# Float32 weights made from float64 by their bits: work moved from VectorE to ScalarE, in blocks of 1024 columns

## Chip, cores and metric

One core of one Trainium2 chip. The metric is device time in microseconds (us) of one execution, median of several; lower is better. All runs quoted here were in the fast state. Engine names as in the profile: PE is TensorE's matmuls, PEld its weight loads, DVE is VectorE, ACT is ScalarE, POOL is GpSimd, SP is SyncE, which issues most transfers here.

## The reference, cut to what matters

Two attention reads (tokens from state, state from tokens) feed a feed-forward block with ELU. The weights arrive as 8-byte words, float64.

```python
def _attn_ref(x, state):            # x 8 x 8 x 512 x 64, state 8 x 8 x 32 x 64
    scores = scale * x @ state^T;   a  = softmax(scores);   xread = a  @ state
    scores2 = scale * state @ x^T;  a2 = softmax(scores2);  sread = a2 @ x
    return concat([xread, sread], axis=2)

def _moe_ref(x, w_in, w_out):       # x 4352 x 512, w_in 512 x 2048, w_out 2048 x 512
    h = x @ w_in
    g = np.where(h > 0.0, h, np.exp(np.minimum(h, 0.0)) - 1.0)
    return g @ w_out
```

## The kernel before

A float64 word is loaded as two 32-bit words, `lo` and `hi`. DVE rebuilds the float32 value with seven instructions per block of 512 columns; there are 16 blocks of w_in and 16 of w_out.

```python
    rawpool = ctx.enter_context(tc.tile_pool(name="raw", bufs=3))
    ...
    w_in = cpool.tile([P, NP, DF], FP32, name="w_in")
    w_out = cpool.tile([P, FO, DM], FP32, name="w_out")
    v_bd = cpool.tile([P, B * G, P], FP32, name="v_bd")
    k_bd = cpool.tile([P, B * G, P], FP32, name="k_bd")
    ...

    def setup():
        nc.vector.memset(v_bd, 0.0)
        make_identity(nc, ident)
        s_v = state.rearrange("b (g h) n d -> h n (b g) d", h=4)
        for h in range(4):
            c = h % 2
            nc.gpsimd.dma_start(
                out=v_bd[h * NS : (h + 1) * NS, :, c * D : (c + 1) * D], in_=s_v[h]
            )
        for b in range(2):
            load_x(b)
        for k in range(0, B * G, 4):
            ps = bank([P, 4, P], "k_ps")
            for i in range(4):
                nc.tensor.transpose(ps[:, i], v_bd[:, k + i], ident)
            nc.vector.tensor_copy(out=k_bd[:, k : k + 4], in_=ps)
    ...
    def load_weights(dst, src):


        raw = rawpool.tile([P, 512], moe_w_in.dtype, name="raw")
        k = src.shape[-1]
        nc.sync.dma_start(out=raw.rearrange("p (j k) -> p j k", k=k), in_=src)
        words = raw.bitcast(U32).rearrange("p (j k w) -> p j k w", k=k, w=2)
        lo, hi = words[:, :, :, 0], words[:, :, :, 1]
        power = wpool.tile([P, 512], U32, name="power").rearrange("p (j k) -> p j k", k=k)

        nc.vector.tensor_scalar(
            out=power, in0=hi, scalar1=20, scalar2=0x7FF,
            op0=ALU.logical_shift_right, op1=ALU.bitwise_and,
        )
        low = 1023 - 127
        nc.vector.tensor_scalar(
            out=power, in0=power, scalar1=float(low), scalar2=float(low + 255),
            op0=ALU.max, op1=ALU.min,
        )
        nc.vector.tensor_scalar(
            out=power, in0=power, scalar1=float(-low), scalar2=float(1 << 23),
            op0=ALU.add, op1=ALU.mult,
        )
        nc.vector.scalar_tensor_tensor(
            out=power, in0=hi, scalar=0x80000000, in1=power,
            op0=ALU.bitwise_and, op1=ALU.bitwise_or,
        )

        nc.vector.tensor_scalar(
            out=hi, in0=hi, scalar1=0xFFFFF, scalar2=0x100000,
            op0=ALU.bitwise_and, op1=ALU.bitwise_or,
        )
        nc.vector.scalar_tensor_tensor(
            out=dst, in0=lo, scalar=2.0**-32, in1=hi, op0=ALU.mult, op1=ALU.add
        )
        nc.vector.scalar_tensor_tensor(
            out=dst, in0=dst, scalar=2.0**-20, in1=power.bitcast(FP32),
            op0=ALU.mult, op1=ALU.mult,
        )
```

Its users: `make_m` multiplies k_bd with one chunk (512 columns) of w_in, two rows of the tile per m_ps bank, and `ffn1` of a batch needs m for its chunk; `ffn2` needs w_out.

```python
        for g in range(G):
            ps = bank([P, 512], "m_ps")
            for i in range(2):
                nc.tensor.matmul(
                    ps[i * D : (i + 1) * D],
                    k_bd[:, b * G + g, i * D : (i + 1) * D],
                    w_in[:, 2 * g + i, c * 512 : (c + 1) * 512],
                    start=True, stop=True,
                )
    ...
    setup()
    todo = [lambda c=c, n=n: load_w_in(c, n) for c in range(FC) for n in range(NP)]
    for f in attention(0):
        f()
        if todo:
            todo.pop(0)()
    ...
    make_m(0, 0)
```

The order of instructions in each engine's queue is not the order of this text: it is fixed at compile time, so an edit in one place can also move instructions elsewhere (w_out_cheap below shows a case). Names that end in `_ps` are tiles in PSUM; every matmul of this kernel writes one, `h_ps` in `ffn1` and `o_ps` in `ffn2`.

Of the kernel before, what the change touches and what calls it, by code (L numbers as in the profile page):

```python
# [2 lines left out]

# [6 lines left out]
FP32 = mybir.dt.float32  # L10
I32 = mybir.dt.int32
U32 = mybir.dt.uint32
AX_X = mybir.AxisListType.X
AF = mybir.ActivationFunctionType
ALU = mybir.AluOpType
PSUM = bass.MemoryType.PSUM


@with_exitstack
def kernel(  # L20
# [11 lines left out]
    nc = tc.nc  # L32

    B, H, S, D = x.shape
    NS = state.shape[2]
    DM, DF = moe_w_in.shape
    P = 128
    R = S // P
    NP = H // 2
    G = H // 4  # L40
    FO = DF // P
    FC = DF // 512
    SB = S + NS
    NB = S // 32
    scale = 1.0 / math.sqrt(D)
# [7 lines left out]
    w_in_v = moe_w_in.rearrange("(co ci) f -> ci co f", ci=P)  # L53
    w_out_v = moe_w_out.rearrange("(fo fi) c -> fi fo c", fi=P)

    cpool = ctx.enter_context(tc.tile_pool(name="const", bufs=1))
# [2 lines left out]
    xtpool = ctx.enter_context(tc.tile_pool(name="xT", bufs=4))  # L59
    atpool = ctx.enter_context(tc.tile_pool(name="aT", bufs=4))  # L60
    mpool = ctx.enter_context(tc.tile_pool(name="m", bufs=2))
    rawpool = ctx.enter_context(tc.tile_pool(name="raw", bufs=3))
    wpool = ctx.enter_context(tc.tile_pool(name="pow", bufs=2))
    small = ctx.enter_context(tc.tile_pool(name="small", bufs=4))
    gpool = ctx.enter_context(tc.tile_pool(name="g", bufs=FO + 1))
# [1 line left out]
    opool = ctx.enter_context(tc.tile_pool(name="o", bufs=2))  # L67
    ps_a = ctx.enter_context(tc.tile_pool(name="ps_a", bufs=3, space=PSUM))
    ps_h = ctx.enter_context(tc.tile_pool(name="ps_h", bufs=3, space=PSUM))
    ps_o = ctx.enter_context(tc.tile_pool(name="ps_o", bufs=2, space=PSUM))  # L70

# [7 lines left out]
    w_in = cpool.tile([P, NP, DF], FP32, name="w_in")  # L79
    w_out = cpool.tile([P, FO, DM], FP32, name="w_out")  # L80


    v_bd = cpool.tile([P, B * G, P], FP32, name="v_bd")

    k_bd = cpool.tile([P, B * G, P], FP32, name="k_bd")

# [12 lines left out]
# [17 lines that stand above are left out]
    def load_weights(dst, src):  # L116


        raw = rawpool.tile([P, 512], moe_w_in.dtype, name="raw")
        k = src.shape[-1]  # L120
        nc.sync.dma_start(out=raw.rearrange("p (j k) -> p j k", k=k), in_=src)
        words = raw.bitcast(U32).rearrange("p (j k w) -> p j k w", k=k, w=2)
        lo, hi = words[:, :, :, 0], words[:, :, :, 1]
        power = wpool.tile([P, 512], U32, name="power").rearrange("p (j k) -> p j k", k=k)

        nc.vector.tensor_scalar(  # L126
            out=power, in0=hi, scalar1=20, scalar2=0x7FF,
            op0=ALU.logical_shift_right, op1=ALU.bitwise_and,
        )
        low = 1023 - 127  # L130
        nc.vector.tensor_scalar(  # L131
            out=power, in0=power, scalar1=float(low), scalar2=float(low + 255),
            op0=ALU.max, op1=ALU.min,
        )
        nc.vector.tensor_scalar(  # L135
            out=power, in0=power, scalar1=float(-low), scalar2=float(1 << 23),
            op0=ALU.add, op1=ALU.mult,
        )
        nc.vector.scalar_tensor_tensor(  # L139
            out=power, in0=hi, scalar=0x80000000, in1=power,  # L140
            op0=ALU.bitwise_and, op1=ALU.bitwise_or,
        )

        nc.vector.tensor_scalar(  # L144
            out=hi, in0=hi, scalar1=0xFFFFF, scalar2=0x100000,
            op0=ALU.bitwise_and, op1=ALU.bitwise_or,
        )
        nc.vector.scalar_tensor_tensor(  # L148
            out=dst, in0=lo, scalar=2.0**-32, in1=hi, op0=ALU.mult, op1=ALU.add
        )  # L150
        nc.vector.scalar_tensor_tensor(  # L151
            out=dst, in0=dst, scalar=2.0**-20, in1=power.bitcast(FP32),
            op0=ALU.mult, op1=ALU.mult,
        )
    def load_w_in(c, n):
        cols = slice(c * 512, (c + 1) * 512)
        load_weights(w_in[:, n : n + 1, cols], w_in_v[:, n : n + 1, cols])

    def load_w_out(fo):
        load_weights(w_out[:, fo : fo + 1], w_out_v[:, fo : fo + 1])  # L160

    def turn_x(b, g, i):

# [83 lines left out]
    def make_m(b, c):  # L247

        m_t[b, c] = mpool.tile([P, G, 512], FP32, name="m_sb")
# [7 lines that stand above are left out]
                    start=True,  # L257
                    stop=True,
                )
            (nc.scalar.copy, nc.vector.tensor_copy)[g % 2](out=m_t[b, c][:, g], in_=ps)  # L260

    def attention(b):
        steps = []
        for g in range(G):
            steps += [lambda g=g, i=i: turn_x(b, g, i) for i in range(2)]
            steps += [lambda g=g: scores(b, g)]
        for g in range(G):
            steps += [lambda g=g: turn_tokens(b, g)]
            steps += [lambda g=g: turn_state(b, g)]
            steps += [lambda g=g: state_read(b, g)]  # L270
        if b + 2 < B:
            steps += [lambda: load_x(b + 2)]
        return steps
# [12 lines left out]
    def ffn1(g, b, fo):  # L286

        ps = ps_h.tile([P, S], FP32, tag="h", name="h_ps")
        for k in range(G):
            nc.tensor.matmul(  # L290
                ps,
                m_t[b, fo // 4][:, k, fo % 4 * P : (fo % 4 + 1) * P],
                st[b, k, "aT"],
                start=(k == 0),
                stop=(k == G - 1),
            )
        elu(ps, g, fo)
# [14 lines left out]
    def ffn2(g, c, o_sb):  # L312
        ps = ps_o.tile([P, DM], FP32, tag="o", name="o_ps")
        for fo in range(FO):
            nc.tensor.matmul(  # L315
                ps,
                g[fo][:, c * P : (c + 1) * P],
                w_out[:, fo],
                start=(fo == 0),
                stop=(fo == FO - 1),  # L320
            )
        (nc.scalar.copy, nc.vector.tensor_copy)[c % 2](out=o_sb[:, c % 2], in_=ps)  # L322

    setup()
    todo = [lambda c=c, n=n: load_w_in(c, n) for c in range(FC) for n in range(NP)]
    for f in attention(0):
        f()
        if todo:
# [4 lines left out]
    for b in range(B):  # L333
        todo = attention(b + 1) if b + 1 < B else []
        g = {}
        for fo in range(FO):
            ffn1(g, b, fo)
            if fo % 4 == 1 and fo // 4 + 1 < FC:
                make_m(b, fo // 4 + 1)
            if b == 0:  # L340
                load_w_out(fo)
            if todo:
                todo.pop(0)()
        rows = out_b[b, 0:S].rearrange("(p r) c -> p r c", r=R)
        for c in range(R):
            if c % 2 == 0:
                o_sb = opool.tile([P, 2, DM], FP32, name="o_sb")
            ffn2(g, c, o_sb)
            if c % 2:
                nc.sync.dma_start(out=rows[:, c - 1 : c + 1], in_=o_sb)  # L350
            if todo:
                todo.pop(0)()
            if c == 2 and b + 1 < B:
                make_m(b + 1, 0)
        for f in todo:
            f()
# [5 lines left out]
    for c in range(2):  # L362
        ffn2(g, c, o_sb)
        for i in range(P // NS):
            nc.sync.dma_start(
                out=out_b[c * (P // NS) + i, S:SB], in_=o_sb[i * NS : (i + 1) * NS, c]
# [31 lines left out]
```

## Time and profile before

| | before |
|---|---|
| median of 3 runs | 932.17 us |
| span of the profiled run | 931.1 us |
| PE busy, idle | 872.7, 58.4 us |
| DVE busy, ACT busy | 363.1, 156.9 us |
| PE dense from | 88.4 us |
| last w_out block converted | 165 us |

Up to 88 us PE waits much; afterwards it is nearly always busy. The prediction shows the lines.

### The profile page before, as it was taken

To read this page: it belongs to the slowest core of one execution; us is meant where nothing else is said; L and a number is where in the kernel's file an instruction comes from. 1 tells how busy PE (TensorE), PEld (TensorE's weight loads), DVE (VectorE), ACT (ScalarE), POOL (GpSimd) and SP (SyncE) were. 2 spreads that over 40 slices of the span, in tenths; PEclk is the share of its full clock that TensorE was granted. 3 is DMA by queue.
4 is the path that set the end of the run, shared out by engine and by line. 5 is a ranking of instruction groups with operands and counts; after the bars stand their busy time and mean duration, and the time that the engine had idled before them with its cause. 6 is when DMAs were issued, how large, how long until landed. Compare 5 with 4: busy or idle time off the path is not lost.

```text
span 931.1 us, 6560 instructions
## 1 busy us (share of the span) xinstructions
PE 872.7 (94%) x2512; PEld 401.3 (43%) x2512; DVE 363.1 (39%) x774; ACT 156.9 (17%) x290; POOL 53.1 (6%) x58
## 2 busy tenths in 40 slices
PE   1474999999999999999999999999999999999997
PEld 1331443445444444444444444454444444444673
DVE  3989999435004610272017400660036102500220
ACT  0211211123003300141004200330023101300110
POOL 3110110001000200010001000000001000000000
PEclk9966999999999999999999999999999999999999
DMA  8354242002000110002000200000000000000000
GB/s 200 109 148 153 90 136 91 23 23 46 1 23 23 25 21 23 23 0 46 23 23 0 46 23 1 23 1 1 23 24 0 1 23 23 0 1 23 23 0 23
DMA packets 25439, 35.01 MB, mean 38 GB/s; under 512 B 17857, under 2 KB 17857, under 8 KB 25409
## 3 DMA queue, kind: packets, MB, share of 16 engines
q1 hardware_dynamic: 23936, 29.89, 10.4%
q0 software_dynamic: 1472, 4.72, 2.3%
q8 instruction: 19, 0.31, 0.1%
q14 instruction: 12, 0.09, 0.0%
HBM read 25.69 MB, written 8.91 MB: 37 GB/s over the span
## 4 chain that ended last, share of the span: by engine, by line
PE 88%; DVE 8%; DMA 3%; SPq 1%; ACT 0%; issue 0%; POOL 0%; DVEq 0%; ACTq 0%
PE o_ps L315 49%; PE h_ps L290 23%; PE m_ps L253 6%; PE h_ps L303 3%; DMA raw<-in_moe_w_in_dram 3%; PE sr_ps L233 3%; PE s_ps L175 2%; PE xT_ps L166 2%; DVE power L139 1%; DVE w_in L148 1%; DVE power L126 1%; DVE raw L144 1%; PE sT_ps L224 1%; DVE power L131 1%; DVE power L135 1%; DVE w_in L151 0%
## 5 line engine op out<-in xcount | busy, mean ns | idle before, releaser
L315 PE MATMUL o_ps<-w_out,g_sb 128*128 128x512 f32 x1088 | 473.6, 594 | 0.0
L315 PEld LDWEIGHTS o_ps<-w_out,g_sb 128*128 128x128 f32 x1088 | 205.3, 190 | 263.0 <-issue 256.3
L290 PE MATMUL h_ps<-aT,m_sb 128*128 128x512 f32 x512 | 242.1, 606 | 12.8 <-DVE m_sb L260 12.6
L290 PEld LDWEIGHTS h_ps<-aT,m_sb 128*128 128x128 f32 x512 | 92.3, 193 | 123.1 <-issue 82.7
L279 ACT ACTIVATE e_sb<-h_ps 128x512 f32<-128x512 f32 (+1 forms) x144 | 82.4, 572 | 335.4 <-PE h_ps L290 295.9
L322 DVE COPY o_sb<-o_ps 128x512 f32<-128x512 f32 x17 | 11.7, 690 | 323.6 <-PE o_ps L315 323.6
L282 DVE SCALAR_TENSOR_TENSOR g_sb<-e_sb,h_ps 128x512 f32<-128x512 f32 (+1 forms) x144 | 93.7, 651 | 11.6 <-PE o_ps L315 8.6
L280 DVE TENSOR_SCALAR e_sb<-e_sb 128x512 f32<-128x512 f32 (+1 forms) x144 | 59.0, 410 | 98.4 <-ACT e_sb L279 98.4
L253 PE MATMUL m_ps<-w_in,k_bd 128*64 128x512 f32 x256 | 68.1, 622 | 1.5 <-ACT xT L168 0.8
L322 ACT COPY o_sb<-o_ps 128x512 f32<-128x512 f32 x17 | 10.0, 586 | 304.5 <-PE o_ps L315 304.5
L260 DVE COPY m_sb<-m_ps 128x512 f32<-128x512 f32 x32 | 22.0, 688 | 91.0 <-PE m_ps L253 89.5
L199 POOL TENSOR_TENSOR t_sb<-t_sb,top_t 128x512 f32<-128x512 f32 x16 | 17.8, 1115 | 570.0 <-DVE top_t L198 445.4
L233 PEld LDWEIGHTS sr_ps<-aT_s,x_sb 128*128 128x128 f32 x256 | 33.9, 209 | 10.9 <-ACT aT_s L226 6.4
L253 PEld LDWEIGHTS m_ps<-w_in,k_bd 128*64 128x64 f32 x256 | 15.8, 138 | 46.5 <-issue 35.3
L233 PE MATMUL sr_ps<-aT_s,x_sb 128*128 128x64 f32 x256 | 34.5, 292 | 1.4 <-ACT aT_s L226 1.3
L113 PE MATMUL k_ps<-ident,v_bd 128*128 128x128 f32 x16 | 3.9, 426 | 29.8 <-DVE k_bd L114 16.6
L303 PE MATMUL h_ps<-xT_state,w_in 128*128 128x256 f32 x128 | 27.8, 379 | 0.0
L168 ACT COPY xT<-xT_ps 128x512 f32<-128x512 f32 x32 | 18.6, 584 | 52.6 <-PE xT_ps L166 52.6
L166 PEld LDWEIGHTS xT_ps<-ident,x_sb 128*128 128x128 f32 x128 | 16.6, 151 | 22.5 <-issue 12.1
L303 PEld LDWEIGHTS h_ps<-xT_state,w_in 128*128 128x128 f32 x128 | 24.3, 190 | 3.7 <-issue 0.5
L166 PE MATMUL xT_ps<-ident,x_sb 128*128 128x128 f32 x128 | 21.4, 295 | 3.1 <-DVE xT_state L242 3.0
L260 ACT COPY m_sb<-m_ps 128x512 f32<-128x512 f32 x32 | 18.8, 586 | 22.9 <-PE m_ps L253 22.9
(42 smaller groups left out, 328.7 us busy)
## 6 DMA issues: line engine op xcount, KB each, us to landing
raw<-in_moe_w_in_dram SPq DMA_DIRECT2D x16, 512.0 KB, 4.2
raw<-in_moe_w_out_dram SPq DMA_DIRECT2D x16, 512.0 KB, 3.3
out_dram<-o_sb SPq DMA_DIRECT2D x16, 512.0 KB, 2.6
x_sb<-in_x_dram SPq DMA_DIRECT2D x16, 256.0 KB, 4.8
x_sb<-in_x_dram POOLq DMA_DIRECT2D x16, 256.0 KB, 5.9
v_bd<-in_state_dram POOLq DMA_DIRECT2D x4, 128.0 KB, 7.6
out_dram<-o_sb SPq DMA_DIRECT2D x8, 64.0 KB, 1.7
```

What stands on the lines that cost most here:

```text
L166: nc.tensor.transpose(ps[:, r], x_t[b][:, r, (2 * g + i) * P : (2 * g + i + 1) * P], ident)
L175: nc.tensor.matmul(ps[i * D : (i + 1) * D], k_bd[:, b * G + g, i * D : (i + 1) * D], st[b, g, i], start=True, stop=True,)
L233: nc.tensor.matmul(ps[:, i], x_t[b][:, r, (2 * g + i) * P : (2 * g + i + 1) * P], st[b, g, "aT_s"][:, r, i * D : (i + 1) * D], start=(r == 0),
L253: nc.tensor.matmul(ps[i * D : (i + 1) * D], k_bd[:, b * G + g, i * D : (i + 1) * D], w_in[:, 2 * g + i, c * 512 : (c + 1) * 512], start=Tr ...
L260: (nc.scalar.copy, nc.vector.tensor_copy)[g % 2](out=m_t[b, c][:, g], in_=ps)
L279: nc.scalar.activation(out=e, in_=ps, func=AF.Exp)
L280: nc.vector.tensor_scalar(out=e, in0=e, scalar1=1.0, scalar2=None, op0=ALU.min)
L282: nc.vector.scalar_tensor_tensor(out=g[fo], in0=e, scalar=-1.0, in1=ps, op0=ALU.add, op1=ALU.max)
L290: nc.tensor.matmul(ps, m_t[b, fo // 4][:, k, fo % 4 * P : (fo % 4 + 1) * P], st[b, k, "aT"], start=(k == 0), stop=(k == G - 1),)
L303: nc.tensor.matmul(ps, w_in[:, co, fo * P : (fo + 1) * P], xT_state[:, co], start=(co == 0), stop=(co == NP - 1),)
L315: nc.tensor.matmul(ps, g[fo][:, c * P : (c + 1) * P], w_out[:, fo], start=(fo == 0), stop=(fo == FO - 1),)
L322: (nc.scalar.copy, nc.vector.tensor_copy)[c % 2](out=o_sb[:, c % 2], in_=ps)
```

## The change

The intent: relieve DVE, which is full from 18 to 165 us. ACT rounds the low word and takes the absolute value of the high word; DVE clamps, shifts, sets the sign and adds two integers. Blocks double in size to spread fixed costs: 1024 columns, which for w_in are two rows of 512. Memory for that comes from two raw buffers in place of three, with v_bd lying in one of them.

```diff
-    rawpool = ctx.enter_context(tc.tile_pool(name="raw", bufs=3))
+    rawpool = ctx.enter_context(tc.tile_pool(name="raw", bufs=2))
...
-    v_bd = cpool.tile([P, B * G, P], FP32, name="v_bd")
+    v_bd = rawpool.tile([P, B * G, P], FP32, tag="raw", name="v_bd")
...
-        (seven DVE instructions per 512 columns)
+        ulps = wpool.tile([P, 1024], FP32, name="ulps")
+        nc.scalar.activation(out=ulps, in_=lo, func=AF.Copy, scale=2.0**-29, bias=2.0**23)
+        nc.scalar.activation(
+            out=ulps.bitcast(U32), in_=ulps, func=AF.Copy, bias=-(2.0**23)
+        )
+        nc.scalar.activation(
+            out=dst, in_=hi.bitcast(FP32).rearrange("p (j k) -> p j k", k=k), func=AF.Abs
+        )
         nc.vector.tensor_scalar(
+            out=dst, in0=dst, scalar1=as_float(896 << 20),
+            scalar2=as_float((1151 << 20) - 1), op0=ALU.max, op1=ALU.min,
+        )
+        bits = dst.bitcast(U32)
+        nc.vector.tensor_scalar(
+            out=bits, in0=bits, scalar1=3, scalar2=0x3FFFFFF8,
+            op0=ALU.logical_shift_left, op1=ALU.bitwise_and,
+        )
         nc.vector.scalar_tensor_tensor(
+            out=bits, in0=hi.rearrange("p (j k) -> p j k", k=k), scalar=0xC0000000, in1=bits,
             op0=ALU.bitwise_and, op1=ALU.bitwise_or,
         )
+        nc.vector.tensor_tensor(
+            out=bits, in0=bits,
+            in1=ulps.bitcast(U32).rearrange("p (j k) -> p j k", k=k), op=ALU.add,
+        )
...
-        load_weights(w_in[:, n : n + 1, cols], w_in_v[:, n : n + 1, cols])
+        load_weights(w_in[:, n : n + 2, cols], w_in_v[:, n : n + 2, cols])
```

More of the change, by code (lines that the diff above doesn't have):

```diff
@@ L1 @@
 import math
+import struct
 from contextlib import ExitStack
@@ L16, with as_float @@
 PSUM = bass.MemoryType.PSUM
+def as_float(bits):
+    return struct.unpack("f", struct.pack("I", bits))[0]
 @with_exitstack
@@ L116, in load_weights @@
     def load_weights(dst, src):
-        raw = rawpool.tile([P, 512], moe_w_in.dtype, name="raw")
         k = src.shape[-1]
+        raw = rawpool.tile([P, 1024], moe_w_in.dtype, tag="raw", name="raw")
         nc.sync.dma_start(out=raw.rearrange("p (j k) -> p j k", k=k), in_=src)
-        words = raw.bitcast(U32).rearrange("p (j k w) -> p j k w", k=k, w=2)
-        lo, hi = words[:, :, :, 0], words[:, :, :, 1]
-        power = wpool.tile([P, 512], U32, name="power").rearrange("p (j k) -> p j k", k=k)
@@ L126, in load_weights @@
-        nc.vector.tensor_scalar(
-            out=power, in0=hi, scalar1=20, scalar2=0x7FF,
-            op0=ALU.logical_shift_right, op1=ALU.bitwise_and,
-        )
-        low = 1023 - 127
-        nc.vector.tensor_scalar(
-            out=power, in0=power, scalar1=float(low), scalar2=float(low + 255),
-            op0=ALU.max, op1=ALU.min,
+        words = raw.bitcast(U32).rearrange("p (j w) -> p j w", w=2)
+        lo, hi = words[:, :, 0], words[:, :, 1]
+        ulps = wpool.tile([P, 1024], FP32, name="ulps")
@@ L134, in load_weights @@
+        nc.scalar.activation(out=ulps, in_=lo, func=AF.Copy, scale=2.0**-29, bias=2.0**23)
+        nc.scalar.activation(
+            out=ulps.bitcast(U32), in_=ulps, func=AF.Copy, bias=-(2.0**23)
+        )
+        nc.scalar.activation(
+            out=dst, in_=hi.bitcast(FP32).rearrange("p (j k) -> p j k", k=k), func=AF.Abs
         )
         nc.vector.tensor_scalar(
-            out=power, in0=power, scalar1=float(-low), scalar2=float(1 << 23),
-            op0=ALU.add, op1=ALU.mult,
+            out=dst, in0=dst, scalar1=as_float(896 << 20),
+            scalar2=as_float((1151 << 20) - 1), op0=ALU.max, op1=ALU.min,
+        )
@@ L138, in load_weights @@
+        bits = dst.bitcast(U32)
+        nc.vector.tensor_scalar(
+            out=bits, in0=bits, scalar1=3, scalar2=0x3FFFFFF8,
+            op0=ALU.logical_shift_left, op1=ALU.bitwise_and,
         )
         nc.vector.scalar_tensor_tensor(
-            out=power, in0=hi, scalar=0x80000000, in1=power,
+            out=bits, in0=hi.rearrange("p (j k) -> p j k", k=k), scalar=0xC0000000, in1=bits,
             op0=ALU.bitwise_and, op1=ALU.bitwise_or,
         )
-        nc.vector.tensor_scalar(
-            out=hi, in0=hi, scalar1=0xFFFFF, scalar2=0x100000,
-            op0=ALU.bitwise_and, op1=ALU.bitwise_or,
-        )
@@ L148, in load_weights @@
-        nc.vector.scalar_tensor_tensor(
-            out=dst, in0=lo, scalar=2.0**-32, in1=hi, op0=ALU.mult, op1=ALU.add
-        )
-        nc.vector.scalar_tensor_tensor(
-            out=dst, in0=dst, scalar=2.0**-20, in1=power.bitcast(FP32),
-            op0=ALU.mult, op1=ALU.mult,
+        nc.vector.tensor_tensor(
+            out=bits,
+            in0=bits,
+            in1=ulps.bitcast(U32).rearrange("p (j k) -> p j k", k=k),
+            op=ALU.add,
         )
@@ L156, in load_w_in @@
         cols = slice(c * 512, (c + 1) * 512)
-        load_weights(w_in[:, n : n + 1, cols], w_in_v[:, n : n + 1, cols])
+        load_weights(w_in[:, n : n + 2, cols], w_in_v[:, n : n + 2, cols])
     def load_w_out(fo):
-        load_weights(w_out[:, fo : fo + 1], w_out_v[:, fo : fo + 1])
+        load_weights(w_out[:, fo : fo + 2], w_out_v[:, fo : fo + 2])
     def turn_x(b, g, i):
@@ L324 @@
     setup()
-    todo = [lambda c=c, n=n: load_w_in(c, n) for c in range(FC) for n in range(NP)]
+    todo = [lambda c=c, n=n: load_w_in(c, n) for c in range(FC) for n in range(0, NP, 2)]
     for f in attention(0):
@@ L339 @@
                 make_m(b, fo // 4 + 1)
-            if b == 0:
+            if b == 0 and fo % 2 == 0:
                 load_w_out(fo)
```

## The prediction

> **What bounds the kernel now.** I read the page's busy shares and slices first, because one average over 931 us mixes a start with a long steady part.
>
> ```profile
> PE 872.7 (94%) x2512; PEld 401.3 (43%) x2512; DVE 363.1 (39%) x774; ACT 156.9 (17%) x290; POOL 53.1 (6%) x58
> ...
> PE   1474999999999999999999999999999999999997
> ...
> DVE  3989999435004610272017400660036102500220
> ACT  0211211123003300141004200330023101300110
> ...
> PEclk9966999999999999999999999999999999999999
> ```
>
> PE is full from the fifth slice (93 us) on. DVE is full only in slices 2 to 7, ACT never. So nothing done to DVE or ACT helps after about 168 us; the conversion of the weights lies before that. The windows view, cut where PE becomes dense (88.4) and where the last w_out block is converted and PE runs o_ps without a break (168.1), gives the stages (columns: length, busy us of PE, PEld, DVE, ACT, POOL, then PE clock, DMA share, GB/s):
>
> ```profile
> 0.00:34.00 34.00, 4.08 (x17) 3.31 (x18) 19.11 (x39) 1.28 (x1) 7.01 (x14) 1.00 0.74 185
> 34.00:88.40 54.40, 33.69 (x104) 17.22 (x104) 49.87 (x114) 9.70 (x19) 7.11 (x6) 0.65 0.47 135
> 88.40:168.10 79.70, 76.58 (x221) 31.65 (x222) 77.23 (x171) 17.60 (x32) 6.42 (x6) 1.00 0.32 99
> 168.10:931.10 763.00, 758.36 (x2173) 349.13 (x2171) 216.85 (x453) 128.31 (x239) 32.59 (x32) 1.00 0.06 18
> ```
>
> The last 763 us are matmuls and can't move. Of PE's 58 us of idle time, 51 lie before 88.4, and there it also ran at a mean clock of 0.65. The waits say who kept PE idle:
>
> ```profile
> DVE power L126 <- DMA raw<-in_moe_w_in_dram: 17.5, 5, 12.2
> ...
> PE k_ps L113 <- DVE k_bd L114: 16.6, 1, 16.6
> ...
> PE h_ps L290 <- DVE m_sb L260: 12.6, 1, 12.6
> ```
>
> The two PE waits are for a short DVE copy out of PSUM that stood in DVE's queue behind blocks of conversion: k_bd copied at 31.9 us although its transposes ran at 13.3 to 16.0, m_sb copied at 82.7 although its matmuls ended by 64. DVE itself waited for data only 17.5 us in all, 12.2 of them for the first block. From 18.6 to 165 us **DVE's conversion is the bound**, and PE fills what it can beside it.
>
> How much is conversion: seven instructions per 512-column block, 32 blocks. Four are of the short kind, three of the long kind (groups view of DVE up to 165 us; the other four lines are alike), and the timeline gives the distance from start to start:
>
> ```profile
> L139 DVE SCALAR_TENSOR_TENSOR power<-raw,power 128x512 uint32<-128x512 uint32 x32 | 22.0, 688 | 0.1
> ...
> L131 DVE TENSOR_SCALAR power<-power 128x512 uint32<-128x512 uint32 x32 | 13.5, 423 | 0.0
> ...
> L148 DVE SCALAR_TENSOR_TENSOR w_in<-raw 128x512 f32<-128x512 uint32 x16 | 10.9, 683 | 0.0
> ```
>
> ```profile
> 22.45 0.42 DVE L131 TENSOR_SCALAR power<-power 128x512 uint32<-128x512 uint32 x1
> 22.79 0.68 DVE L148 SCALAR_TENSOR_TENSOR w_in<-raw 128x512 f32<-128x512 uint32 x1
> 23.39 0.42 DVE L135 TENSOR_SCALAR power<-power 128x512 uint32<-128x512 uint32 x1
> 23.72 0.68 DVE L151 SCALAR_TENSOR_TENSOR w_in<-w_in,power 128x512 f32<-128x512 f32 x1
> ```
>
> One record lasts 0.42 or 0.68 us, but the next starts 0.34 or 0.60 us later. I count with these distances. A block is 4 x 0.34 + 3 x 0.60 = 3.16 us, 32 blocks 101 us, of the 146 us from 18.6 to 165.
>
> **What the Trainium skill says.** (1) "VectorE: DVE Perf Modes", section on the perf-mode tier table: a float32 tensor_scalar within SBUF runs at two elements a cycle, a tensor_tensor at one. The trace agrees: 512 elements take 0.34 against 0.60 us. (2) "ScalarE: Activation LUTs", section "What ACT_TABLE_LOAD costs": an activation with immediate scale and bias takes 186 ns + 0.833 ns per column. The trace has one operation at two widths:
>
> ```profile
> L279 ACT ACTIVATE e_sb<-h_ps 128x512 f32<-128x512 f32 x128 | 76.2, 595 | 300.4 <-PE h_ps L290 295.9 <-DVE raw L144 4.0
> ...
> L279 ACT ACTIVATE e_sb<-h_ps 128x256 f32<-128x256 f32 x16 | 6.1, 384 | 35.0 <-PE h_ps L303 35.0
> ```
>
> (595 - 384) / 256 = 0.82 ns, which agrees. (3) The same page, section "Table sets: the hidden batching unit": copy and abs are in every set, so the new functions should cause no table load; the trace before shows one load, of 1283 ns, which fits but doesn't prove it for abs. (4) "TensorE: Matmul & The Clock Gate", Part 1: the array runs at half rate until it has been busy for some microseconds. The clock of 0.65 from 34 to 88 against 1.00 afterwards agrees, so denser early work should also run faster.
>
> **The change, part by part.** It removes all seven DVE instructions per 512 columns. Per 1024 columns it adds:
> - DVE: two tensor_scalar (clamp; shift and mask), one scalar_tensor_tensor (sign), one tensor_tensor (add). Doubling the columns adds 512 elements: 0.267 us to the short kind and 0.533 us to the long, from 0.34 to 0.60 and from 0.60 to 1.13 us. A block is 2 x 0.60 + 2 x 1.13 = 3.5 us; 16 blocks are 55 us. **DVE is relieved of 101 - 55 = 46 us.**
> - ACT: three activations. From the row above, 595 + 512 x 0.82 = 1.02 us each, 3.0 us a block, 49 us in all. ACT is busy 27 us between 34 and 168, so with 49 it remains below DVE's load; its total rises from 157 to about 206.
> - DMA: the same bytes in 16 transfers of 1 MB rather than 32 of 512 KB. The 3.3 us to landing of this row become some 5.5 (estimate: another 512 KB at the 240 to 300 GB/s seen while only weights move).
>
> ```profile
> raw<-in_moe_w_out_dram SPq DMA_DIRECT2D x16, 512.0 KB, 3.3
> ```
>
> - Buffers: two of 1 MB for raw, and v_bd lies in one of them. The second weight transfer so waits until the k_ps transposes have read v_bd, and the fourth group of these needs a k_bd copy. The order of DVE's queue must therefore put k_bd ahead of the second block. I expect these copies at 17 to 20 us rather than 32 to 33, and attention starts some 13 us sooner.
>
> The pace. A raw buffer is held for three activations (3.0), two tensor_scalar (1.3) and the sign (1.2), about 5.6 us from landing, then a transfer of 5.5 to 6 us refills it. A cycle of 11.3 us on two buffers is a block each 5.7 us if no other work delays it. Block 0 lands near 15 us and block 1 near 24; fourteen more at 5.7 give 107 us for the last of w_out, at 6.5 with attention and ELU work in between about 118. I take **T = 118 instead of 165**. That is also what subtracting 46 us of DVE work gives, so two routes agree.
>
> What PE must still do then. Before 168.1 it did (start-to-start times at full clock: 0.43 us per 512-column matmul, 0.23 for m_ps, 0.22 for s_ps, 0.11 for the small ones) 76 h_ps, 61 o_ps, 48 m_ps, 20 s_ps and 136 small ones: 33 + 26 + 11 + 4 + 15 = 89 us. By 118 it can't have done it all: only two o_ps banks accumulate (32 matmuls per bank pair, 14 us), and the 17 g buffers stop h_ps of the second batch after one chunk, so about 75 us of work are to be had; with attention's latency and cold clock at the start I take 72. The end is 118 + 3 (last matmuls, as 165 to 168 now) + 763 + (89 - 72) = 901 us of span; the timed run is 1 us above the span. **Predicted: 901 us**, 31 us (3.3%) less.
>
> **Rivals.** (a) *The two buffers and the transfer become the bound.* Each block's chain (transfer, ACT, DVE) is serial per buffer, and DVE would idle waiting for ACT. If delays in both queues stretch 5.7 to 8 us, T is 24 + 14 x 8 = 136 plus conversion of 5, and with 78 us of PE work done the end is 141 + 3 + 763 + 11 = 918. For it: three smaller buffers shrink to two, one blocked at first. Against it: bandwidth is at 135 GB/s in the second stage, far from what it reaches. (b) *ACT's queue becomes the one that blocks.* ACT works in order, and xT, aT_s and exp copies behind an activation that waits for a transfer hold PE up, as DVE's m_sb copy does now. Then PE does only 60 us by T = 118: 118 + 3 + 763 + 29 = 913. For it: exactly this happened on DVE. Against it: ACT has slack of more than half. (c) *PE is bound by its own work from the start:* if k_bd and w_in come early enough and fill work is found, 80 us are done by T = 105, and the end is 105 + 3 + 763 + 9 = 880. For it: PE was 96% busy beside the last w_out blocks. Against it: softmax's latency, 19 us from the first xT to the last sr_ps now. (d) *Abs needs a table load*: 32 loads of 1.28 us on ACT, partly hidden, about 10 us worse; I give it 5%.
>
> **Range and chances.** Centre 901; (c) and a mild (a) or (b) bound it: 882 to 919, eight times in ten. Faster by over 2% means under 913.5: the centre clears it by 12, (a) and the worst of (b) miss it: 0.78. Within 2%: 0.2. Slower needs both queues blocking with PE starved throughout: 0.02.
>
> **What would show it.** Right if: DVE busy falls by about 50 us and ACT rises by about 49 with still one table load; the new DVE records are near 0.69 and 1.21 us, activations near 1.02; k_bd copies before 21 us; the last write of w_out near 118; dense o_ps afterwards and unchanged PE work. Wrong if strided or integer operands make a new instruction slower than its row, if DVE or ACT shows long waits for raw after 30 us, or if PE waits for ACT's xT or exp in place of DVE's m_sb.

## The result, and the profile after

The changed kernel takes **923.52 us** (median of 4 runs, 922.93 to 924.61) against 932.17 us (4 runs) for the kernel before. The ratio of their fast runs is 0.9909, with a 95% interval of 0.9892 to 0.9926: 0.9% less, where 3.3% was predicted. Ratios here are the mean time of one kernel's fast runs over that of the other's in the same rounds, so not quite the ratio of the medians. The result is correct.

The page's shares and slices after:

```profile
PE 868.9 (94%) x2512; PEld 400.9 (43%) x2512; DVE 319.4 (35%) x614; ACT 203.7 (22%) x338; POOL 53.9 (6%) x58
...
PE   1368999999999999999999999999999999999997
...
DVE  2678990173006500461017300740046002500220
ACT  1547650141004300231014100420033001300110
...
PEclk8658999999999999999999999999999999999999
```

DVE lost 43.7 us and ACT gained 46.8, as planned, and DVE is full only in slices 5 and 6. But PE's first four slices read 1368 where they read 1474. The windows view, cut where PE becomes dense (75.7) and 763 us ahead of the end:

```profile
0.00:34.00 34.00, 6.33 (x25) 5.00 (x26) 10.43 (x12) 8.43 (x9) 7.01 (x14) 0.76 0.61 148
34.00:75.70 41.70, 22.73 (x70) 12.17 (x68) 32.72 (x50) 24.16 (x31) 7.07 (x6) 0.62 0.59 194
75.70:159.30 83.60, 82.34 (x237) 35.99 (x237) 58.83 (x97) 40.32 (x55) 7.25 (x6) 1.00 0.32 107
159.30:922.30 763.00, 757.51 (x2184) 347.74 (x2182) 217.45 (x456) 130.80 (x244) 32.61 (x32) 1.00 0.06 17
```

PE is dense 12.7 us sooner than before, but has then done no h_ps at all, where before it had done 12. Of the 8.8 us by which the span fell, 5.0 are less idle time of PE (58.4 to 53.4) and 3.8 less busy time. Two waits hold PE:

```profile
PE k_ps L119 <- DVE k_bd L120: 15.8, 1, 15.8
...
PE m_ps L261 <- DVE w_in L156: 7.6, 1, 7.6
```

The first is nearly as long as before (16.6). The chain of work that ended last (start, length, what) shows why:

```profile
20.39 1.24 DVE w_in L152
21.64 0.05 issue
21.69 5.16 DMA raw<-in_moe_w_in_dram
26.87 1.12 ACT ulps L133
27.99 1.02 ACT w_in L139
29.04 0.69 DVE w_in L142
29.73 0.60 DVE k_bd L120
```

Block 1's transfer starts when block 0's last reader (L152, the sign) is done: it took **block 0's** buffer, not v_bd's. Block 1's first DVE instruction (L142) stands ahead of k_bd in DVE's queue, so attention waits for a whole transfer and conversion.

The second wait is new. PE's timeline:

```profile
63.43 1.07 PE L261 MATMUL m_ps<-w_in,k_bd 128*64 128x512 f32 x2 [0.68 <-ACT xT L176]
72.13 3.67 PE L261 MATMUL m_ps<-w_in,k_bd 128*64 128x512 f32 x4 [7.63 <-DVE w_in L156]
75.73 2.07 PE L298 MATMUL h_ps<-aT,m_sb 128*128 128x512 f32 x4
```

The integer add (L156) that releases m_ps at 72.13 is that of the seventh block, which belongs to the last chunk of w_in. But m_ps is there making m of the first chunk, whose two blocks were ready by 38 us. The next m_ps matmuls start when the add of the eighth block, also of the last chunk, ends at 77.9:

```profile
76.66 1.23 DVE L156 CUSTOM_DVE_ANT_0 w_in<-w_in,ulps 128x2048 uint16<-128x2048 uint16 x1
...
77.94 0.20 PEld L261 LDWEIGHTS m_ps<-w_in,k_bd 128*64 128x64 f32 x4 [0.96 <-DVE w_in L156]
```

### The profile page after: what moved, and what is told of

Its sections match the earlier page's. It is cut to its first block, busy times and chain, and to the rows that moved or that the text cites. A ratio compares the mean times of both kernels' runs of the same rounds, so it can differ in the third digit from the quotient of the medians.

```text
span 922.3 us, 6441 instructions
## 1 busy us (share of the span) xinstructions
PE 868.9 (94%) x2512; PEld 400.9 (43%) x2512; DVE 319.4 (35%) x614; ACT 203.7 (22%) x338; POOL 53.9 (6%) x58
## 4 chain that ended last, share of the span: by engine, by line
PE 91%; DMA 3%; DVE 3%; ACT 2%; SPq 0%; issue 0%; ACTq 0%; DVEq 0%
PE o_ps L323 51%; PE h_ps L298 24%; PE m_ps L261 7%; DMA raw<-in_moe_w_in_dram 3%; PE sr_ps L241 3%; PE h_ps L311 3%; PE s_ps L183 2%; PE xT_ps L174 2%; PE sT_ps L232 1%; ACT ulps L133 1%; ACT w_in L139 0%; DVE w_in L152 0%; DVE w_in L142 0%; SPq L101 0%; DVE e_sb L288 0%; DVE w_in L148 0%
## 5 line engine op out<-in xcount | busy, mean ns | idle before, releaser
L298 PE MATMUL h_ps<-aT,m_sb 128*128 128x512 f32 x512 | 238.2, 599 | 1.1 <-DVE m_sb L268 0.8
L261 PE MATMUL m_ps<-w_in,k_bd 128*64 128x512 f32 x256 | 70.2, 621 | 8.5 <-DVE w_in L156 7.6
L261 PEld LDWEIGHTS m_ps<-w_in,k_bd 128*64 128x64 f32 x256 | 16.6, 138 | 54.9 <-issue 37.4
L311 PEld LDWEIGHTS h_ps<-xT_state,w_in 128*128 128x128 f32 x128 | 24.3, 190 | 3.7 <-issue 0.5
L133 ACT ACTIVATE ulps<-raw 128x1024 f32<-128x1024 uint32 x16 | 18.3, 1143 | 34.2 <-DMA raw<-in_moe_w_in_dram 32.9
L174 PEld LDWEIGHTS xT_ps<-ident,x_sb 128*128 128x128 f32 x128 | 15.9, 147 | 19.4 <-issue 11.8
L268 ACT COPY m_sb<-m_ps 128x512 f32<-128x512 f32 x32 | 18.8, 587 | 13.9 <-PE m_ps L261 13.9
L176 ACT COPY xT<-xT_ps 128x512 f32<-128x512 f32 x32 | 18.6, 585 | 13.9 <-PE xT_ps L174 13.9
```

What stands on the lines that cost most here:

```text
L133: nc.scalar.activation(out=ulps, in_=lo, func=AF.Copy, scale=2.0**-29, bias=2.0**23)
L174: nc.tensor.transpose(ps[:, r], x_t[b][:, r, (2 * g + i) * P : (2 * g + i + 1) * P], ident)
L261: nc.tensor.matmul(ps[i * D : (i + 1) * D], k_bd[:, b * G + g, i * D : (i + 1) * D], w_in[:, 2 * g + i, c * 512 : (c + 1) * 512], start=Tr ...
L268: (nc.scalar.copy, nc.vector.tensor_copy)[g % 2](out=m_t[b, c][:, g], in_=ps)
L298: nc.tensor.matmul(ps, m_t[b, fo // 4][:, k, fo % 4 * P : (fo % 4 + 1) * P], st[b, k, "aT"], start=(k == 0), stop=(k == G - 1),)
L311: nc.tensor.matmul(ps, w_in[:, co, fo * P : (fo + 1) * P], xT_state[:, co], start=(co == 0), stop=(co == NP - 1),)
```

## The experiments

Each kernel is compared by its ratio to the kernel before, run on the same chip in the same rounds (932.15 to 932.19 us there). The changed kernel's own ratio is 0.9909.

| run | median us | ratio to before | 95% interval |
|---|---|---|---|
| w_in_by_chunk | 913.49 | 0.9807 | 0.9790 to 0.9824 |
| kbd_first | 912.71 | 0.9801 | 0.9784 to 0.9818 |
| vbd_away | 915.48 | 0.9823 | 0.9809 to 0.9837 |
| w_out_cheap (wrong on purpose) | 921.68 | 0.9894 | 0.9879 to 0.9909 |
| new_512 | 911.06 | 0.9776 | 0.9763 to 0.9790 |
| old_1024 | 932.46 | 1.0007 | 0.9995 to 1.0020 |
| old_kbd_first | 931.11 | 0.9993 | 0.9979 to 1.0007 |
| chunk_kbd_vbd | 905.79 | 0.9721 | 0.9702 to 0.9740 |
| add_by_row | 913.37 | 0.9797 | 0.9784 to 0.9810 |
| chunk_kbd | 903.14 | 0.9692 | 0.9679 to 0.9706 |
| new_512_kbd | 905.31 | 0.9715 | 0.9701 to 0.9728 |
| all_cheap (wrong on purpose) | 882.73 | 0.9470 | 0.9457 to 0.9483 |

My theory after reading the trace: the arithmetic did its work, and two things gave most of it back, a false wait (a wait for data that the waiting instruction does not read) for later chunks of w_in, and the late k_bd copies. The rival was that two raw buffers set the pace whatever one does.

### w_in_by_chunk: the layout of w_in

```diff
-    w_in = cpool.tile([P, NP, DF], FP32, name="w_in")
+    w_in = cpool.tile([P, FC, NP, 512], FP32, name="w_in")
```

A block becomes one unbroken stretch of 1024; the two places that read w_in are indexed to match.

> Only the layout of w_in changes, so that a block of two rows by 512 columns is one unbroken stretch. Theory (false wait): in the changed kernel a block is written with a hole between its two rows, and the second matmul of each m_ps pair waits for blocks of later chunks whose stretch covers its row, so ffn1 of the first batch can't start before all of w_in is converted. Then here the 7.6 us wait of m_ps for w_in is gone, the first h_ps starts near 62 us rather than 75.7, and the time falls by 6 to 14 us, to 910 to 918. Rival (pace of two raw buffers): w_in arrives no sooner, the first h_ps moves but PE idles as long later; within 2 us of 923.5.

Measured: 913.49 us, 1.0% under the changed kernel (0.9807 / 0.9909 = 0.9897). The wait for w_in is gone. PE's timeline:

```profile
57.60 3.68 PE L261 MATMUL m_ps<-w_in,k_bd 128*64 128x512 f32 x8
61.21 1.03 PE L174 MATMUL xT_ps<-ident,x_sb 128*128 128x128 f32 x4
62.17 1.08 PE L261 MATMUL m_ps<-w_in,k_bd 128*64 128x512 f32 x4
63.18 3.70 PE L298 MATMUL h_ps<-aT,m_sb 128*128 128x512 f32 x8
```

All eight m_ps matmuls of the first chunk run in one go, and ffn1 starts at 63.2 rather than 75.7 us. The rival's figure (within 2 us of 923.5) is missed by far.

### kbd_first: the order of DVE's queue

```diff
+        with tc.issue_after(k_done[-1].ins):      # the last k_bd copy
             nc.vector.tensor_scalar(out=dst, in0=dst, ... op0=ALU.max, op1=ALU.min)
```

This fixes only the order in the queue, with no wait added.

> The k_bd copies are queued on DVE ahead of the first block. My prediction's step (attention can start by 17 to 20 us if only the queue's order allows it) expects the first xT near 16 to 18 us rather than 31.6, the third transfer issued some 14 us sooner, and 5 to 12 us less in all. Rival (false wait on the whole of w_in): attention ends sooner but ffn1 of the first batch waits for the last block of w_in anyway; only what comes from earlier transfers is won, 0 to 5 us.

Measured: 912.71 us, 1.1% under the changed kernel (0.9801 / 0.9909 = 0.9891). The k_bd copies ran at 12.7 to 15.9 us, the first xT at 15.0, and the first m_ps at 45.1 rather than 58.4. Part of what was won was lost again in the false wait, which grew from 7.6 us:

```profile
PE m_ps L264 <- DVE w_in L159: 11.4, 1, 11.4
```

The gain is at the upper end of the first theory all the same: with k_bd early v_bd is free early, and the second transfer, which takes its buffer here as I had assumed, starts at 15.3 rather than 21.7 us. So the last w_in block came sooner, and ffn1 started at 65.4. One part of the expectation was missed: the third transfer started at 24.3 rather than 31.5 us, 7 us sooner and not 14.

### vbd_away: v_bd out of the raw buffers

```diff
-    v_bd = rawpool.tile([P, B * G, P], FP32, tag="raw", name="v_bd")
+    v_bd = w_out[:, 12:16].rearrange("p a (k q) -> p (a k) q", q=P)
```

> v_bd lies in the last quarter of w_out, which is written much later, so both raw buffers are free from the start. Theory (the shared buffer made the first two transfers serial): block 1 is converted right after block 0, some 8 us sooner than 26.9, all of w_in some 5 to 8 us sooner, time lower by 3 to 8 us. Rival (DVE's order): k_bd copies slip behind more blocks, attention starts later than 31.6, and the time is the same or worse.

Measured: 915.48 us. Block 1's first activation ran at 20.2 rather than 26.9 us, as the theory has it, while the k_bd copies stayed at 29.5. The first h_ps came at 65.3. Sharing the buffer costs some 0.9% in the changed kernel; what it delays is w_in, not attention. With w_in sooner the false wait was 1.9 us instead of 7.6, so this gain and that of w_in_by_chunk may be partly the same; no run joins these two alone.

### w_out_cheap: does the end follow the last w_out block?

```diff
+        if (this block is of w_out):
+            nc.vector.tensor_scalar(out=dst, in0=hi.bitcast(FP32)..., scalar1=0.5, op0=ALU.mult)
+            return
```

> Wrong result on purpose: w_out is made by one DVE instruction per block from the high word, so 24 activations and 24 DVE instructions are gone, all transfers stay. My prediction's formula (the end follows the last w_out block, T) expects T to move from 139 to about 115 and the time to fall by some 20 us, to 900 to 908. Rival (PE is dense from 76 us on, whenever w_out comes): T moves as much, but the time stays within 4 us of 923.5.

Measured: 921.68 us. The view of the tile w_out has its writers (duration min/median/max in ns, first and last start in us):

```profile
L133 DVE TENSOR_SCALAR w_out<-raw x8: 654/684/1458, 78.3 to 107.9; 128x1024 f32<-128x1024 f32 x8
```

The last write moved from 139 us to 109, and the time by less than 2 us. **My formula's T is not what ends this kernel**: PE has other work to do from 76 us on. It was busy for 69.3 of the 70 us from 90 to 160 here, and for 69.7 of them in the changed kernel, so that an earlier w_out had no idle time to fill. The edit also changed PE's order (first o_ps at 119.3 us here, at 95.3 in the changed kernel); what that alone did was not tested.

### new_512, old_1024, old_kbd_first: arithmetic and blocks apart

new_512 is the new arithmetic with 512-column blocks, three raw buffers and v_bd in its own place. old_1024 is the old arithmetic with the changed kernel's blocks and buffers. old_kbd_first is the kernel before with `issue_after` as in kbd_first.

> The new arithmetic in the blocks and buffers of the kernel before: 512 unbroken columns, three raw buffers, v_bd in its own place. Theory (the block of two rows and the shared buffer cost what the arithmetic won): no m_ps waits for a later chunk, no serial second transfer, and the time is 903 to 914, below the changed kernel by 10 us or more. Rival (the new chain through ACT and DVE is too slow for any buffers): within 3 us of 923.5 or above it.

> The old arithmetic of seven DVE instructions in the blocks and buffers of the changed kernel: two rows of 512, two raw buffers, v_bd in one of them. Theory (false wait and sharing cost time by themselves): the second m_ps half waits for the last blocks of w_in, which DVE now finishes near 85 us, so the time is above 932, 936 to 955. Rival (the blocks are neutral, the arithmetic gives all of the 9 us): within 3 us of 932.

> The kernel before with the k_bd copies queued on DVE ahead of its first block. Theory (the start of attention is a matter of DVE's queue order, whichever arithmetic is used): first xT near 15 us, time 921 to 928. Rival (DVE has no idle time from 18 to 165 us in the kernel before, so its order moves nothing): within 2 us of 932.

Measured: 911.06, 932.46 and 931.11 us. The new arithmetic is worth 2.2% in the old blocks but 0.9% in the new ones. For the other two **my theory failed and the rival held**: with the old arithmetic neither the blocks nor the order of k_bd matter. DVE is busy 69.8 of the 70 us from 90 to 160 in old_1024; when a queue is full all the time, what comes first in it does not change when it is done. That is my reading; the runs show only that the times are equal.

old_1024 also refuted a part of my explanation. Its w_in blocks are written with the same hole, yet its second m_ps halves wait for nothing new, and its first h_ps ran at 69.6 us, before w_in was complete at 88. So the hole alone is not the cause. What differs is the last writer of a block. The integer add is a special instruction in the trace (DVE groups up to 200 us of the changed kernel):

```profile
L152 DVE SCALAR_TENSOR_TENSOR w_in<-raw,w_in 128x1024 uint32<-128x1024 uint32 x8 | 9.8, 1222 | 0.2
L156 DVE CUSTOM_DVE_ANT_0 w_in<-w_in,ulps 128x2048 uint16<-128x2048 uint16 x8 | 9.8, 1220 | 0.5
...
L142 DVE TENSOR_SCALAR w_in<-w_in 128x1024 f32<-128x1024 f32 x8 | 8.3, 1032 | 27.4 <-ACT w_in L139 27.4
```

### add_by_row: the add alone

```diff
-        nc.vector.tensor_tensor(out=bits, in0=bits, in1=(all of ulps), op=ALU.add)
+        for j in range(1024 // k):
+            nc.vector.tensor_tensor(out=bits[:, j], in0=bits[:, j],
+                                    in1=(row j of ulps), op=ALU.add)
```

> Only the last DVE step of a block changes: the integer add is issued once per row of 512 (two instructions for a block of w_in) rather than once over both rows. Theory (narrowed after the run of the old arithmetic in the new blocks, in which m_ps waited for no later chunk: it is the add's own instruction whose written stretch is taken without its hole): m_ps no longer waits 7.6 us for a later block, and the time is that of the run with w_in laid out by chunk, 911 to 917. Rival (that run's gain came from something else in its layout, such as faster reading of rows by TensorE): within 3 us of 923.5.

Measured: 913.37 us, the time of w_in_by_chunk (ratios 0.9797 and 0.9807, intervals overlapping). The wait of m_ps for w_in is not in the trace. So the false wait is that of the add's instruction alone, when it covers two rows with a hole between them.

### chunk_kbd, chunk_kbd_vbd, new_512_kbd: the mends together

chunk_kbd joins w_in_by_chunk and kbd_first; chunk_kbd_vbd adds vbd_away; new_512_kbd is new_512 with k_bd first and four raw buffers.

> The changed kernel with all three mends: w_in laid out by chunk, k_bd queued first, v_bd away from the raw buffers. If the three costs are separate they add up to some 29 us and the time is 893 to 900; if they hide each other, as the waits of one chain do (attention sooner, then the false wait longer, 11.4 us in the run with k_bd first), somewhere from 898 to 906. My prediction's 901 would then be the value of the arithmetic without the three costs. Rival: nothing more than the best single one, 910 to 913.

> w_in by chunk and k_bd first, v_bd still in a raw buffer. With k_bd first, v_bd is free by 15 us, before block 0 is even converted, so sharing should cost nothing more: within 2 us of 905.8, the time with all three mends. Rival: ACT takes only one block ahead of attention's xT copies here instead of two, so attention runs sooner and it is 2 to 5 us faster than 905.8.

> New arithmetic in blocks of 512, four raw buffers, v_bd in its own place, k_bd first. Shorter blocks hold ACT and DVE for half as long, so attention's copies and reductions wait less in the queues than in the run with all three mends: 897 to 905. Rival (the extra fixed cost of 24 more instructions of each kind and the shorter transfers eat that): 905 to 911.

Measured: 905.79, **903.14** and 905.31 us. The two mends add up: 0.9897 times 0.9891 is 0.9789, and chunk_kbd against the changed kernel is 0.9692 / 0.9909 = 0.9781. v_bd's place is worth nothing once k_bd is first: all three mends are no better than two, 0.3% worse by the ratios, with intervals that just overlap. The wait for an xT copy, which stands behind two blocks in ACT's queue there instead of one, is 6.9 us in chunk_kbd_vbd and 3.1 in chunk_kbd; that fits the rival, but I made no run that changes this wait alone. new_512_kbd is at the edge of its first theory: shorter blocks win nothing over chunk_kbd. (Its expectation miscounts: 16 more blocks are 48 more activations and 64 more DVE instructions.)

chunk_kbd is faster than both kernels of this case, 3.1% under the kernel before. Its PE slices start fuller:

```profile
PE   3598999999999999999999999999999999999997
```

### all_cheap: what transfers and attention leave

As w_out_cheap, for all weights, with k_bd first.

> Wrong result on purpose: w_in and w_out both made by one DVE instruction per block, k_bd first, buffers as in the changed kernel. It shows what transfers and attention alone leave: my prediction's rival (c), PE bound by its own work, would be reached, 880 to 890. If transfers set the pace of w_in, which then ends near 55 us, the time stays at 895 or more.

Measured: 882.73 us. Its page:

```profile
PE 858.2 (98%) x2512; PEld 398.7 (45%) x2512; DVE 271.0 (31%) x566; ACT 156.1 (18%) x290; POOL 52.7 (6%) x58
```

The same transfers into the same two buffers, each held for one instruction, bring all of w_in by 47 us, and PE is 98% busy. So the transfers themselves do not set the changed kernel's time. Of its 923.5 us, 20.4 are the two unseen costs (to 903.1), and another 20.4 (to 882.7) are the conversion: its time on ACT and DVE, its places in their queues, and the time for which it holds the buffers.

## Why the prediction was wrong

Its range began at 882 and ended at 919; the time is 923.5. By its own steps:

- **The arithmetic and its costs: right.** DVE busy fell by 43.7 us (46 predicted), ACT rose by 46.8 (49). The new records are 0.68 us (tensor_scalar), 1.21 to 1.22 (sign) and 1.22 to 1.25 (add) against 0.69 and 1.21 expected, so that 512 more columns cost 0.26 and 0.54 us where I had estimated 0.267 and 0.533; the activations 1.06 to 1.15 against 1.02. There was one table load, so rival (d) did not occur. Transfers landed in 5.7 and 4.9 us (5.5 to 6). The clamp of w_in averaged 1.03 us rather than 0.68, 2.8 us in all: its three longest records, 1.45 to 1.54 us, each overlap a GpSimd instruction (the one from 41.57, for example, one from 41.34 to 42.56), and the clamps of w_out averaged 0.68; I didn't test the cause.
- **"k_bd at 17 to 20 us": failed.** They were copied at 29.6 us. I assumed that the second transfer takes v_bd's buffer, so that the queue must put k_bd ahead of block 1. It took block 0's buffer (the third took v_bd's), and k_bd stood behind block 1. kbd_first shows the size, 1.1%, 10.8 us by the medians.
- **A wait that I didn't see: the false one.** No step or rival of mine had it; (a), the buffers' pace, came nearest in time (918) but by another mechanism. Two runs give its size, 10.0 and 10.2 us by the medians (w_in_by_chunk, add_by_row).
- **"The end follows T": failed as a mechanism.** T was 139, not 118, and with T = 139 my formula needs only 72 us of PE work done by then, the very figure I took, to give 922. That looks like a confirmation with one mis-sized term. w_out_cheap refutes it: T fell by 30 us and the time by 2. What ends this kernel is when PE becomes dense and what it has done by then: it began late, at 76 us, and from 90 to 160 it was busy for 69.7 of 70 us with T at 139 and for 69.3 with T at 109. PE waited for w_out only in runs in which it started sooner (3.4 us in w_in_by_chunk), and not in all of these (not in chunk_kbd).
- **The pace of a block: too short.** 5.7 us, or 6.5 with other work, were predicted; from the first activation of block 0 (16.8) to that of the last w_in block (71.7) it was 54.9 / 7 = 7.8 us. vbd_away and kbd_first show that much of it is the first transfers, made one after the other. DVE waited 27.4 us for ACT's w_in, and ACT 32.9 us for transfers of w_in (14.7 of them for the first). So DVE was no longer full, and my second route to T, 165 less DVE's 46 us, failed with the first; that the two agreed proved nothing.
- **Rival (b), ACT's queue: partly there.** sr_ps waited 6.1 us for ACT's aT_s, against 1.3 in the kernel before. I have not tested it alone.
- **Two readings in the sum of PE's work.** I counted 32 matmuls, 14 us, for two o_ps banks. The trace has 32 records, 13.9 us, for one bank, and 61 of them had run by 168.1 in the kernel before; so two banks leave more work to be had than I said. And I took the clock of 0.65 as that of a PE with little work, but the row above it reads 1.00 with PE busy for 4.1 of 34 us; after the change it was 0.76 and 0.62 up to 75.7 us, so the hope of a faster early clock did not come true.
- **Rival (c), 880 us: reached only without the conversion** (all_cheap, 882.7).

With both mends the kernel takes 903.1 us, k_bd is copied at 13 to 16 and w_out ends at 121 us, all close to the prediction. The two unseen costs are thus the 20 us that were missing, and the value that I put on the arithmetic was about right. That 901 comes so near to 903.1 may be in part luck: no wait of PE for w_out stands in that trace, so its end is not shown to follow T either. What stays open is how the remaining 20 us of conversion split among these. The waits of PE for a_s (6.0), g_sb (5.2), aT_s (4.3) and xT (3.1) in chunk_kbd name candidates; none was tested by itself.

## What to carry to other kernels

When a loaded engine is relieved, look next at what was hidden behind it: here the order of k_bd in the queue cost nothing while DVE was full (old_kbd_first), and 10.8 us once it was not (kbd_first). The false wait, 10 us, was not hidden before: it came with the new add (old_1024 has the same blocks and no such wait). When a block changes shape, compare the waits of its readers with the data that they read; a matmul that waits for a later chunk than its own is a false wait, and an unbroken layout or one instruction per row takes it away. A formula that fits the time is not yet the cause: remove the term that it rests on and see whether the time moves.

## What the Trainium skill lacked or had wrong

- "VectorE: DVE Perf Modes", section "Specifications", says that integer operands are converted to float32, "exact only below 2^24". It doesn't mention the form that this kernel's uint32 add takes: a custom instruction over 2048 uint16 for 1024 words. It took 1.22 us, as long as the sign instruction over 1024 uint32 (1.22). The results were correct to the test's tolerance; no run here tests exactness.
- No page that I read says how a framework records what such an instruction writes: over two rows with a hole it made readers of other blocks wait, 7.6 us here and 10 us of time.
- "ScalarE: Activation LUTs", section "What ACT_TABLE_LOAD costs", gives 186 ns + 0.833 ns per column with immediates, which is 1.04 us for 1024 columns. The activation with unbroken input took 1.06 us, which agrees. The two that read every second word took 1.12 to 1.15 us; the page has no term for a strided input. No run separates the stride from what else differs between the three.
